# Joining the score matmuls of an attention pair: two of them wait for the exponentials that free both PSUM score tiles

## The chip, the cores and the metric

The kernel runs on one NeuronCore of a Trainium2 chip. The metric is the device time of one execution in microseconds (us). Three runs of the kernel before took 1133.21, 1135.22 and 1140.99 us; the median is 1135.22 us.

## What is computed

Causal attention in blocks of 64 positions, followed by a bilinear feed-forward layer (FFN). There are 8 batches of 8 heads with 576 positions of 64 dimensions. All arrays are float32.

```python
scores = scale * np.matmul(q, k.transpose(0, 1, 3, 2))
mask = block_i >= block_j                       # blocks of 64 positions
scores = np.where(mask, scores, -1000000000.0)
attn = np.exp(scores - np.max(scores, axis=-1, keepdims=True))
attn = attn / (np.sum(attn, axis=-1, keepdims=True) + 1e-09)
x = (attn @ v).transpose(0, 2, 1, 3).reshape(B * S, H * D)   # 4608 x 512
out = (x @ w_a) * (x @ w_b) @ w_out             # 512 -> 1536 -> 512
```

## The kernel before, in words

**Pairs.** Attention works on pairs of heads: 32 pairs, four to a batch. The two heads of a pair lie on partitions 0 to 63 and 64 to 127, so each score matmul has 64 rows (line 542). From pair 10 on (`NATIVE`), each float32 product is made of three matmuls of split operands; before, it is one float32 product.

**Score tiles.** The queries of a pair fall into four tiles of 128, numbered 0 to 3 (`LAST` is 3), and one block that is called the side tile (`NT`). Their scores live in two PSUM tiles, `x` and `y`, of two banks each, and there is one buffer of each (`ps_sc`, line 304):

- C3 writes score tile 3 to `x`, and C1 writes score tile 1 and the side tile to `y`;
- C2 writes score tile 2 to `x` once it is free again, and C0 writes score tile 0 to `y`.

**Exponentials.** VectorE takes the row maxima (t3, t4, t1, t2, t0; line 568), ScalarE the exponentials (line 595). There are two instructions for each tile, one per head: e3, e4 (the side tile), e1, then e2 and e0. C2 may overwrite `x` when e3 is done; C0 may overwrite `y` when e1 and e4 are done. C3 of the next pair needs `x` back from e2, and its C1 needs `y` back from e0.

**After the exponentials.** VectorE sums and inverts (rc, line 658 and below), GpSimd normalises (line 683), VectorE transposes in blocks (lines 688 and 693), DMAs rearrange (`at`, line 739), and TensorE multiplies by the values (V, line 748, 60 matmuls of 64 output columns). V of pair p waits for C0 of pair p+2, so it is placed right behind it. ScalarE copies the result out and splits it (X, H), GpSimd makes the low part (S).

**The FFN's first pass** on a batch needs S of the batch's four pairs. It runs in two halves of a batch. A half has 96 matmuls for the products with `w_a` and `w_b`, and 48 for the output products of the half before it (line 261, 128 x 128 by 128 x 288). They are issued in groups of four (`mm4`) and fill TensorE wherever attention leaves it free. When the attention's 32 pairs and 14 of these halves are through, `rest()` issues the last batch's halves and the output products that are left. The second pass (line 1160) takes the rest of the time, from about 583 us on.

**The order** of the instructions on every engine is written out by `plan()` ahead of time, from estimated durations (`TOOK`, `LAGS`). It takes the engine and operation that can start first; among the operations that are ready within `look` it takes the smallest key. Attention's keys lie near the slot of the pair (`SLOTS`: 12.0 us for each of the first 12 pairs, 15.2 us after), and an FFN group's key is 1e6, so that groups of the FFN only fill. C3 of a pair can't be planned ahead of the start of its slot (`at=B0`). Every operation on TensorE has a `mode`: 0 for the FFN, transposes and warm-up matmuls, 1 for scores, 2 for V; a change of mode costs `SWITCH` in the plan. The order is fixed once it is planned; on the chip the engines follow it, and semaphores hold the real dependencies.

These lines carry the waits that matter here:

```python
add("C3", PE_, ..., [("ql", p), ("kl", p), ("e3" if single_next else "e2", p - 1)], 0, at=B0, mode=1, ...)
add("C1", PE_, c1, [("C3", p, -LAGS[PE_]), ("ql2", p), *([...] if single_next else [("e0", p - 1)])], 0.1, mode=1, ...)
add("C2", PE_, ..., [("e3", p), ("C1", p, -LAGS[PE_])], 7.0, mode=1, ...)
add("C0", PE_, ..., [("C2", p, -LAGS[PE_]), ("e1", p), ("e4", p)], 7.1, mode=1, ...)
```

Of the kernel before, what the change touches and what calls it, by code (L numbers as in the profile page):

```python
# [35 lines left out]
K2 = 2  # L36
FIRST = 8
WARM_P = 2
PET = 6
A_KEY = 12  # L40
SLOTS = [12.0] * 12 + [15.2] * 20
CONV_AT = [0, 6.8, 13.6, 20.4, 28.2, 36, 43.8, 51.6, 59.4, 67.2, 75, 82.8]
CONV_KEY = 12.0
CONV_LO = True
KEEP_UNTIL, KEEP_EVERY = 66.0, 2.5
SWITCH = 0.1
LAGS = {"PE": 0.24, "DVE": 0.14, "Activation": 0.17, "Pool": 0.1, "SP": 2.0}
TOOK = {
# [41 lines left out]
def attention_then_bilinear_ffn(  # L90
# [222 lines left out]
    nk = [min(P * t + 3 * BLK, S - BLK) for t in range(NT)]  # L313
    ew = [min(P * (t + 2), S - BLK) for t in range(NT)]
    LAST = NT - 1
# [47 lines left out]
    PE_, DVE_, ACT_, POOL_, SP_ = LAGS  # L363
# [12 lines left out]
    def plan(look=0.0):  # L376
        free = dict.fromkeys(LAGS, 0.0)
        ready = {e: [] for e in LAGS}
        users = [[] for _ in ops]
        left = [len(o.deps) for o in ops]  # L380
        for o in ops:
            for d, plus in o.deps:
                users[d.n].append((o, plus))
            if not o.deps:
                ready[o.eng].append(o)
        out = []
        mode = 0
        bus = 0.0
        held = []

        def since(o):
            if not o.frees:
                return o.at
            if len(held) < MM:
                return o.at
            r = held[-MM]
            return o.at if r is o else 1e9 if r.end is None else max(o.at, r.end)

        while any(ready.values()):
            t, e = min((max(free[e], min(map(since, q))), e) for e, q in ready.items() if q)  # L400
            o = min((o for o in ready[e] if since(o) <= t + look), key=lambda o: (o.key, o.n))
            t = max(t, since(o))
            if o.frees:
                held.append(o.frees)
            ready[e].remove(o)
            free[e] = t + o.took + (SWITCH if e == PE_ and o.mode != mode else 0)
            if e == PE_:
                mode = o.mode
            if o.also:
                free[ACT_] = max(free[ACT_], t) + o.also  # L410
            o.start, o.end = t, free[e] + o.lag
            if o.kind in KB:
                bus = max(bus, t + LATENCY - 0.3) + KB[o.kind] / RATE
                o.end = bus + 0.3
            out.append(o)
            for u, plus in users[o.n]:
                u.at = max(u.at, o.end + plus + (SLACK if u.eng == PE_ and e != PE_ else 0))
                left[u.n] -= 1
                if not left[u.n]:
                    ready[u.eng].append(u)  # L420
        assert len(out) == len(ops)
        return out
# [23 lines left out]
    def ends(x):  # L446

        return x.rearrange("p (c k) -> p c k", k=BLK)[:, ::S // BLK - 1]

    def products(p, x, y):  # L450

        if p < NATIVE:
            return [(x[:, 0], y[:, 0])]
        x, y = x.bitcast(F32R), y.bitcast(F32R)
        return [(x[:, 1], y[:, 1]), (x[:, 1], y[:, 0]), (x[:, 0], y[:, 1])]

    base = [sum(SLOTS[:p]) for p in range(len(SLOTS))]
    done = {}

    def got(what, p):  # L460
        return done.get((what, p))

    def attention(p):
# [5 lines left out]
        B0 = base[p]  # L469
# [5 lines left out]
        def add(what, eng, fn, deps=(), off=0.0, kind=None, **kw):  # L475
            deps = [(got(*d[:2]), *d[2:]) if isinstance(d, tuple) else (d,) for d in deps]
            done[what, p] = o = Op(kind or what, eng, fn, [(*d, 0.0)[:2] for d in deps if d[0]], key=B0 + off, **kw)
            return o
# [44 lines left out]
        def bank(x):  # L523
            st[x] = ps_sc.tile([P, 2, 512], F32, tag=x, name=f"{x}{n}_{len(st)}")
            return st[x]
# [11 lines left out]
        def scores(t, out):  # L537
            qk = products(p, heads[p]["q"], heads[p]["k"])
            for j, (qq, kk) in enumerate(qk):
                for h, r in enumerate(rows):  # L540
                    keys = ends(kk[r]) if t == NT else kk[r, :nk[t]]
                    nc.tensor.matmul(  # L542
                        out[h] if isinstance(out, list) else out[:, h], qq[r, q0[t]:q0[t] + P], keys, start=j == 0,
                        stop=j == len(qk) - 1 and not (masked and t != LAST), skip_group_check=masked)
            if masked and t != LAST:
                for h, r in enumerate(rows):
                    to = out[h] if isinstance(out, list) else out[:, h]
                    to, val = (to, neg[r]) if t == NT else (to[:, nk[t] - BLK:nk[t]], neg[r, BLK:])
                    nc.tensor.matmul(to, who[r], val, start=False, stop=True, skip_group_check=True)

        single_next = p and p - 1 < SINGLE
        nat = "m" if masked else "n" if native else ""
        side = slice(nk[1], nk[1] + P)

        def c1():
            y = bank("y")
            scores(NT, y[:, :, side])
            scores(1, y[:, :, :nk[1]])

        add("C3", PE_, lambda: scores(LAST, bank("x")), [("ql", p), ("kl", p), ("e3" if single_next else "e2", p - 1)], 0, at=B0, mode=1, kind=nat + "C3")  # L560
        add("C1", PE_, c1, [("C3", p, -LAGS[PE_]), ("ql2", p), *([("e4", p - 1), ("e1", p - 1)] if single_next else [("e0", p - 1)])], 0.1, mode=1, kind=nat + "C1")

        def tile_small():
# [56 lines left out]
        if single:  # L620
            c1_ = ("C1", p, -LAGS[PE_])
            r2 = Op("none", PE_, lambda: ring(2, 0), [(got("C1", p), -LAGS[PE_])], key=B0 + K2)

            def c2():
                ring(2, 1)
                scores(2, [view(2, h) for h in range(2)])

            o2 = add("C2", PE_, c2, [(r2, 0.0), c1_], K2 + .01, mode=1, kind=nat + "C2")
            def c0():
                ring(0, 1)  # L630
                st[0, 0] = ps_sc.tile([P, 512], F32, tag="av", name=f"s{n}_0_0")
                scores(0, [view(0, h) for h in range(2)])

            o0 = add("C0", PE_, c0, [("C2", p, -LAGS[PE_]), ("X", p - 1)], K2 + .1, mode=1, kind=nat + "C0")
            add("t2", DVE_, lambda: [nc.vector.tensor_reduce(st["nm"][:, h, 2:3], view(2, h), axis=AX.X, op=ALU.max, negate=True) for h in range(2)], [("C2", p), ("t3", p)], K2 + 1, kind="u2")
            add("t0", DVE_, lambda: [nc.vector.tensor_reduce(st["nm"][:, h, :1], view(0, h), axis=AX.X, op=ALU.max, negate=True) for h in range(2)], [("C0", p), ("t3", p)], K2 + 1.2, kind="u0")
        else:
            add("C2", PE_, lambda: scores(2, bank("x")[:, :, :nk[2]]), [("e3", p), ("C1", p, -LAGS[PE_])], 7.0, mode=1, kind=nat + "C2")
            add("C0", PE_, lambda: scores(0, bank("y")[:, :, :nk[0]]),
                [("C2", p, -LAGS[PE_]), ("e1", p), ("e4", p)], 7.1, mode=1, kind=nat + "C0")  # L640
            if masked:
                done["m2", p] = got("C2", p)
            else:
                add("m2", DVE_, lambda: mask(2, "x"), [("C2", p)], 8.0)
            add("t2", DVE_, lambda: top(2, st["x"][:, :, :nk[2]]), [("m2", p)], 8.1)
            if masked:
                done["m0", p] = got("C0", p)
            else:
                add("m0", DVE_, lambda: mask(0, "y"), [("C0", p)], 8.2)
            add("t0", DVE_, lambda: top(0, st["y"][:, :, :nk[0]]), [("m0", p)], 8.3)  # L650
# [72 lines left out]
        for i, t in enumerate((LAST, 2, 1, 0, NT)):  # L723
            for h in range(2):
                prev = add("N", POOL_, lambda t=t, h=h: norm(t, h), [prev, got("rc", p)], 13 + i, kind=f"N{t}")
                if by_pe:
                    o = add("T", PE_, lambda t=t, h=h: pe_turn(t, h), [prev, ("V0", p - 1, -LAGS[PE_])], 14 + i, kind=f"P{t}")
                    o.frees = add("A", ACT_, lambda t=t, h=h: place(t, h), [o, *at_free], A_KEY + i, kind=f"A{t}")
                    ts.append(o.frees)
# [7 lines left out]
        def move(i, g):  # L737
# [4 lines left out]
                 key=B0 + 23) for i in range(NQ) for g in range(NQ)]  # L742
# [27 lines left out]
        for c in range(NCH):  # L770
            o = add("V", PE_, lambda c=c: values(c), vs, 18 if by_pe else 27, mode=2, kind=f"V{c}")
# [241 lines left out]
    while k * KEEP_EVERY < KEEP_UNTIL:  # L1013
        o = Op("keep", PE_, keep_on, at=4 + k * KEEP_EVERY, key=1e5)
# [14 lines left out]
    o = Op("st", SP_, start_conv2, [done["C0", NP - 1], done["V", NP - 1]], key=base[-1] + 10)  # L1029
    for k in range(EARLY):  # L1030
        o = Op("cv1", DVE_, lambda: next(box["g"]), [o, done["rc", NP - 1]], key=base[-1] + 20 + k)
# [526 lines left out]
```

## Time and profile before

| | before |
|---|---|
| median of three runs | 1135.22 us (1133.21 to 1140.99) |
| span of the profiled execution, first to last instruction | 1131.4 us |
| mean granted TensorE clock | 0.997 of full speed |
| TensorE matmul, busy | 1106.5 us, 98% of the span |
| VectorE, busy | 867.4 us, 77% |
| ScalarE, busy | 634.7 us, 56% |
| GpSimd, busy | 407.0 us, 36% |
| last V of the attention ends | 522.6 us |

How to read the profile. PE is TensorE's matmul, PEld its loading of weights, DVE is VectorE, ACT ScalarE, POOL GpSimd, SP the queue that issues most DMAs. A row of the timeline gives the start in us, the time that the row covers, the engine, the line, the operation, output and inputs, and the shape; neighbours of one kind are merged (`x6`). Matmuls are pipelined and their ends are modelled, so two neighbours overlap in the rows: what a piece of work costs TensorE is read from the start of its first matmul to the start of the next piece. For the profiled execution the page gives the span and no other time, so the sum of the prediction is made against the span, and the median lies 3.8 us above it.

### The profile page before, as it was taken

Reading aid. Unit: us, or ns where it says so; the run is one execution under the profiler, and the core shown is the slowest. Engines: PE = TensorE matmul, PEld = TensorE weight load, DVE = VectorE, ACT = ScalarE, POOL = GpSimd, SP = SyncE. Lnnn points to the kernel's source line nnn. Section 1 sums busy time; section 2 is a strip of 40 time slices with the busy share of each in tenths; the row PEclk is TensorE's granted clock in tenths of the full one; section 3 lists DMA queues with packets and bytes.
Section 4 is the critical chain, followed back from the end, with each engine's and each line's share of the span. In section 5 each row is a group of like instructions: output and inputs, shape, how many; then the busy total and the mean of one; then the engine's idle time right before and its main releaser. Section 6 shows DMA issues by size and latency. Waiting matters only on the chain.

```text
span 1131.4 us, 23204 instructions
## 1 busy us (share of the span) xinstructions
PE 1106.5 (98%) x8441; PEld 1040.2 (92%) x8441; DVE 867.4 (77%) x1797; ACT 634.7 (56%) x1632; POOL 407.0 (36%) x602
## 2 busy tenths in 40 slices
PE   8899999999999999999999999999999999999998
PEld 5567888899989998999999999999999999999998
DVE  6877878687678777753999997787874867867857
ACT  6877576566666556643465554545543545545532
POOL 4876667566656667551100120211202112022020
PEclk9999999999999999999999999999999999999999
DMA  5542688888777877857242663845669135055151
GB/s 171 156 145 87 168 242 217 226 227 213 205 222 210 223 210 201 240 159 209 90 146 73 181 179 86 215 121 144 181 217 333 37 76 112 17 96 102 26 98 56
DMA packets 78257, 178.74 MB, mean 158 GB/s; under 512 B 13120, under 2 KB 34624, under 8 KB 78144
## 3 DMA queue, kind: packets, MB, share of 16 engines
q1 hardware_dynamic: 65472, 159.95, 47.2%
q0 software_dynamic: 12672, 17.31, 10.2%
q8 instruction: 67, 1.10, 0.4%
q14 instruction: 46, 0.38, 0.1%
HBM read 80.74 MB, written 48.76 MB: 114 GB/s over the span
## 4 chain that ended last, share of the span: by engine, by line
PE 78%; DVE 6%; DMA 5%; ACT 4%; POOL 3%; SPq 3%; issue 2%; DVEq 0%; ACTq 0%; POOLq 0%
PE bank L1160 47%; PE ps L261 13%; PE pso L261 6%; PE av L748 5%; PE x L542 3%; PE y L542 2%; SPq L739 2%; ACT e L595 2%; POOL e L683 1%; DMA at<-bl 1%; DVE bl L688 1%; DMA qr<-qT 1%; DVE nm L568 1%; PE tp L709 1%; DMA kr<-kT 1%
## 5 line engine op out<-in xcount | busy, mean ns | idle before, releaser
L1160 PE MATMUL bank<-xh,wab 128*128 128x384 f32 x1344 | 350.0, 338 | 0.7 <-DVE t L1077 0.7
L1266 POOL DMA_DIRECT2D outT<-pt x88 | 78.0, 1129 | 468.6 <-ACT pt L1413 277.6
L1160 PEld LDWEIGHTS bank<-xh,wab 128*128 128x128 f32 x1344 | 244.7, 187 | 1.4 <-DVE t L1077 1.0
L1160 PE MATMUL bank<-xl,wab 128*128 128x384 f32 x672 | 227.0, 338 | 0.0
L261 PE MATMUL ps<-xh,wab 128*128 128x288 f32 x1024 | 213.9, 298 | 0.4 <-ACT ob L873 0.3
L261 PEld LDWEIGHTS ps<-xh,wab 128*128 128x128 f32 x1024 | 165.8, 188 | 6.4 <-issue 4.3
L683 POOL TENSOR_SCALAR e<-e,rc 128x512 f32<-128x512 f32 (+3 forms) x256 | 152.7, 616 | 45.3 <-DVE rc L663 45.3
L261 PE MATMUL ps<-xl,wab 128*128 128x288 f32 x512 | 153.3, 299 | 0.0
L1160 PEld LDWEIGHTS bank<-xl,wab 128*128 128x128 f32 x672 | 125.9, 187 | 0.0
L1077 DVE TENSOR_TENSOR u<-bank,u 128x384 f32<-128x384 f32 x156 | 86.7, 556 | 48.4 <-PE bank L1160 45.2
L688 DVE STREAM_TRANSPOSE bl<-e 128x512 f32<-128x512 f32 (+1 forms) x208 | 110.2, 582 | 10.4 <-POOL e L683 8.7
L1160 PE MATMUL bank<-hz,wo 128*128 128x384 f32 x612 | 110.0, 334 | 0.0
L1160 PEld LDWEIGHTS bank<-hz,wo 128*128 128x128 f32 x612 | 106.5, 188 | 0.0
L748 PEld LDWEIGHTS av<-at,v 128*64 128x64 f32 x1920 | 92.2, 137 | 10.3 <-issue 5.0
L748 PE MATMUL av<-at,v 128*64 128x128 f32 (+1 forms) x1920 | 97.2, 258 | 3.9 <-DMA at<-bl 2.7
L261 PE MATMUL pso<-hh,wo 128*128 128x288 f32 x480 | 100.9, 298 | 0.0
L261 PEld LDWEIGHTS ps<-xl,wab 128*128 128x128 f32 x512 | 96.1, 188 | 3.8 <-issue 3.2
L1077 DVE TENSOR_TENSOR t<-bank,t 128x384 f32<-128x384 f32 x96 | 53.3, 556 | 40.5 <-ACT t L1203 20.3
L261 PEld LDWEIGHTS pso<-hh,wo 128*128 128x128 f32 x480 | 77.6, 188 | 4.4 <-issue 4.1
L595 ACT ACTIVATE e<-y,nm 128x320 f32<-128x320 f32 (+1 forms) x126 | 60.9, 487 | 28.3 <-DVE nm L568 22.4
L568 DVE TENSOR_REDUCE nm<-x 128x2 f32<-128x1024 f32 (+1 forms) x63 | 72.1, 1145 | 5.7 <-PE x L542 4.5
L849 POOL TENSOR_TENSOR hl<-hf,hh 128x288 fp32r<-128x288 f32 x56 | 46.2, 825 | 84.0 <-ACT hh L845 81.6
(156 smaller groups left out, 2006.6 us busy)
## 6 DMA issues: line engine op xcount, KB each, us to landing
at<-bl SPq DMA_DIRECT2D x416, 112.0 KB, 2.5
xr<-xd SPq DMA_DIRECT2D x48, 384.0 KB, 4.6
outT<-pt POOLq DMA_DIRECT2D x88, 192.0 KB, 6.4
cv<-wab SPq DMA_DIRECT2D x24, 512.0 KB, 5.5
v<-vm SPq DMA_DIRECT2D x32, 320.0 KB, 3.5
xd<-xf SPq DMA_DIRECT2D x32, 288.0 KB, 2.6
outT<-ob SPq DMA_DIRECT2D x64, 144.0 KB, 2.3
wabd<-st SPq DMA_DIRECT2D x8, 896.0 KB, 5.3
```

The source lines that it names most:

```text
L261: nc.tensor.matmul(ps, w_, d_, start=(i == 0), stop=(i == n - 1))
L542: nc.tensor.matmul(out[h] if isinstance(out, list) else out[:, h], qq[r, q0[t]:q0[t] + P], keys, start=j == 0, stop=j == len(qk) - 1 and n ...
L568: nc.vector.tensor_reduce(st["nm"][:, :, t], view, axis=AX.X, op=ALU.max, negate=True)
L595: nc.scalar.activation(out, src, AF.Exp, bias=bias, accum_out=sm[:, h, t, :1])
L683: nc.gpsimd.tensor_scalar(ev, ev, st["rc"][:, h, t:t + 1], 1.0, op0=ALU.mult, op1=ALU.mult)
L688: nc.vector.transpose(dst, es[h][t].rearrange("p (c g q) -> p c g q", g=NQ, q=QB))
L739: nc.sync.dma_start(st["at"][QB * g:QB * (g + 1), i], bl[QB * i:QB * (i + 1), g])
L748: nc.tensor.matmul(out[d], v[:, h, c], a[:, qs, h, e_], start=start, stop=stop, skip_group_check=True)
L849: nc.gpsimd.tensor_tensor(lo, box2["hf"], f32(hi), op=ALU.subtract)
L1077: return lambda: v.tensor_tensor(o, a, b, op=op)
L1160: nc.tensor.matmul(banks[bk], a, b, start=start and not i, stop=i == 3 * n - 1, skip_group_check=not start)
L1266: do("acc", POOL_, lambda: nc.gpsimd.dma_start(part[o * P:(o + 1) * P, ts], t, accum_op=ALU.add), [name], [("part", o, 2 * tt_ + j)], key= ...
```

## The change

- From pair 8 on (`JOIN`), C2 waits for e1 and e4 as well as for e3, and C3 waits for e0 of the pair before as well as for e2. C2 and C0 then become ready together, and so do C3 and C1.
- In `plan()`, when TensorE is in mode 1 or 2, an operation with a mode that can start within 0.3 us (`STAY`) is taken ahead of anything else, for all pairs.
- The planned cost of a change of mode goes from 0.1 to 0.2 us (`SWITCH`).
- Within C1, score tile 1 comes ahead of the side tile; it was the other way round.
- For pair 0, a dependency is written without its plus of 0.0; that is the same dependency.

```diff
+JOIN = 8
+STAY = 0.3
...
-SWITCH = 0.1
+SWITCH = 0.2
...
             t, e = min((max(free[e], min(map(since, q))), e) for e, q in ready.items() if q)
-            o = min((o for o in ready[e] if since(o) <= t + look), key=lambda o: (o.key, o.n))
+            stay = [o for o in ready[e] if o.mode and since(o) <= t + STAY] if e == PE_ and mode else []
+            o = min(stay or (o for o in ready[e] if since(o) <= t + look), key=lambda o: (o.key, o.n))
...
         def c1():
             y = bank("y")
+            scores(1, y[:, :, :nk[1]])
             scores(NT, y[:, :, side])
-            scores(1, y[:, :, :nk[1]])
...
-        add("C3", PE_, lambda: scores(LAST, bank("x")), [("ql", p), ("kl", p), ("e3" if single_next else "e2", p - 1)], 0, at=B0, mode=1, kind=nat + "C3")
+        add("C3", PE_, lambda: scores(LAST, bank("x")), [("ql", p), ("kl", p), ("e3" if single_next else "e2", p - 1), *([("e0", p - 1)] if p >= JOIN else [])], 0, at=B0, mode=1, kind=nat + "C3")
...
-            o2 = add("C2", PE_, c2, [(r2, 0.0), c1_], K2 + .01, mode=1, kind=nat + "C2")
+            o2 = add("C2", PE_, c2, [r2, c1_], K2 + .01, mode=1, kind=nat + "C2")
...
-            add("C2", PE_, lambda: scores(2, bank("x")[:, :, :nk[2]]), [("e3", p), ("C1", p, -LAGS[PE_])], 7.0, mode=1, kind=nat + "C2")
+            add("C2", PE_, lambda: scores(2, bank("x")[:, :, :nk[2]]), [("e3", p), *([("e1", p), ("e4", p)] if p >= JOIN else []), ("C1", p, -LAGS[PE_])], 7.0, mode=1, kind=nat + "C2")
```

## The prediction, made before the changed kernel ran

> **What bounds the kernel now.** I read the page first: TensorE's matmuls cover 98% of the span, the other engines far less.
>
> ```profile
> span 1131.4 us, 23204 instructions
> PE 1106.5 (98%) x8441; PEld 1040.2 (92%) x8441; DVE 867.4 (77%) x1797; ACT 634.7 (56%) x1632; POOL 407.0 (36%) x602
> ```
>
> So time is won where TensorE needs less for the same work, or idles less. The modelled ends hide what a matmul costs, so the second view is TensorE's timeline, read from start to start. These rows are pair 20's C2 (`x`), one FFN group, and C0 (`y`).
>
> ```profile
> 313.59 0.43 PE L261 MATMUL ps<-xh,wab 128*128 128x288 f32 x2
> ...
> 313.99 0.43 PE L261 MATMUL ps<-xh,wab 128*128 128x288 f32 x2
> 314.35 0.87 PE L542 MATMUL x<-k,q 64*128 64x448 f32 x6
> 315.15 0.40 PE L261 MATMUL ps<-xl,wab 128*128 128x288 f32 x1
> ...
> 315.87 0.58 PE L542 MATMUL y<-k,q 64*128 64x192 f32 x6
> 316.38 0.78 PE L748 MATMUL av<-at,v 128*64 128x64 f32 x12
> ```
>
> In a stream, three FFN matmuls take 0.40 us (313.59 to 313.99), 0.133 each, so a group of four is worth 0.53. Alone between C2 and C0 it takes 0.72: 0.19 more. C2 takes 0.80 and C0 0.51. Pair 11 is one of three where C0 follows C2 directly:
>
> ```profile
> 173.47 0.87 PE L542 MATMUL x<-k,q 64*128 64x448 f32 x6
> 174.18 0.48 PE L542 MATMUL y<-k,q 64*128 64x192 f32 x6
> 174.58 0.53 PE L261 MATMUL ps<-xh,wab 128*128 128x288 f32 x2
> ```
>
> There C2 takes 0.71 and C0 0.40. Split, the three pieces take 0.80 + 0.72 + 0.51 = 2.03; joined they are worth 0.71 + 0.40 + 0.53 = 1.64. **A split between C2 and C0 costs TensorE 0.39 us**: 0.20 in the scores, 0.19 in the FFN piece.
>
> The Trainium skill has a rule against this: by "TensorE: Matmul & The Clock Gate", section "Step-by-step: what each phase is for", the drain of one matmul overlaps the fill of the next, so neighbours are N cycles apart. By that rule alone the order of the pieces costs nothing and the sum below is 0. The trace disagrees, with 0.72 against 0.53 us for the same four matmuls. It sides with the skill's "TensorEngine Tiling (Array Packing)", section "Key Properties": a change of tiling mode drains TensorE.
>
> **The change part by part.** *C2 joined to C0.* Of pairs 8 to 31, an FFN piece stands between C2 and C0 in 21 (all but 11, 30 and 31). The pieces of the first and the last of them, pairs 8 and 29, begin so:
>
> ```profile
> 130.12 0.40 PE L261 MATMUL pso<-hl,wo 128*128 128x288 f32 x1
> ...
> 456.49 0.40 PE L261 MATMUL ps<-xl,wab 128*128 128x288 f32 x1
> ```
>
> No FFN matmul goes; it only moves into a longer stream. The gain is 21 x 0.39 = 8.2 us; I use pair 20's price for pieces of any length, since it belongs to the seams.
>
> *C3 joined to C1.* They are adjacent in most pairs already. FFN stands between them in pairs 11 and 22 only (V in pair 9). Pair 20, then pair 22:
>
> ```profile
> 303.03 3.13 PE L748 MATMUL av<-at,v 128*64 128x64 f32 x60
> 306.09 0.96 PE L542 MATMUL x<-k,q 64*128 64x512 f32 x6
> 306.89 0.93 PE L542 MATMUL y<-k,q 64*128 64x128 f32 x12
> 307.75 0.40 PE L261 MATMUL ps<-xl,wab 128*128 128x288 f32 x1
> ```
>
> ```profile
> 337.05 0.96 PE L542 MATMUL x<-k,q 64*128 64x512 f32 x6
> 337.94 0.53 PE L261 MATMUL pso<-hh,wo 128*128 128x288 f32 x2
> ...
> 338.66 1.04 PE L542 MATMUL y<-k,q 64*128 64x128 f32 x12
> 339.63 0.40 PE L261 MATMUL pso<-hh,wo 128*128 128x288 f32 x1
> ```
>
> Split: 0.89 + 0.72 + 0.97 = 2.58. Joined: 0.80 + 0.86, and 0.53 for the group, 2.19. Again 0.39; two pairs give 0.8 us.
>
> *What the later C3 loses.* In seven pairs, such as 20 above, C3 follows V directly. If C3 waits for e0 too, V will be done first and a piece of FFN will come between, at the 0.19 of a lone piece. V and scores have different shapes (128\*64 and 64\*128), so the seam behind V is paid either way. 7 x 0.19 = 1.3 us lost; the bounds are 0 and, if all 24 pairs that have none today got one, 4.6.
>
> *The new waits.* TensorE takes its instructions in order, so behind a C2 that waits stand C0, V and the FFN; the plan is to fill the time before it with FFN groups instead. What is left of such waits now:
>
> ```profile
> PEld x L542 <- ACT e L595: 5.9, 14, 1.6
> ```
>
> That is 0.42 us each time. The 24 C2 and 24 C3 of the change could each wait so (20 us, 14 more than now), or none (5.9 less). I take no difference: the plan leaves the same spare time ahead of a C2 that waits for e1 as ahead of one that waits for e3.
>
> *The other edits.* `STAY` and `SWITCH` act on pairs 0 to 7 too. There I take nothing, because TensorE waits for work rather than work for TensorE (the FFN row below, first window); what that cover may be worth if it is gone is the 8 matmuls of that row, 1 us either way. The order within C1 changes which shape meets the FFN: at most the 0.10 that an exit to FFN showed in either score tile (C2 0.80 against 0.71), 32 times, 3 us either way; nothing taken, since the number of matmuls and of seams is the same. No DMA, and nothing on SP's or POOL's queue, is added; they shift with the pair.
>
> *How much later the pair gets.* This is the cost side, and the third view: pair 21 on ScalarE and VectorE.
>
> ```profile
> 328.93 0.20 ACT L595 ACTIVATION_READ_ACCUMULATOR e<-x,nb 128x1 f32 x1
> 330.91 0.23 ACT L595 ACTIVATION_READ_ACCUMULATOR e<-y,nm 128x1 f32 x1
> 331.10 0.60 DVE L693 STREAM_TRANSPOSE bl<-e_s 64x128 f32<-64x128 f32 x2
> 331.73 0.17 DVE L580 MEMSET x<- 64x128 f32 x1
> 331.93 1.09 DVE L568 TENSOR_REDUCE nm<-x 128x2 f32<-128x896 f32 x1
> ...
> 337.46 0.24 ACT L595 ACTIVATION_READ_ACCUMULATOR e<-y,nm 128x1 f32 x1
> ```
>
> e3 ends at 329.13, e1 at 331.14: C2 becomes ready 2.0 us later. It started at 329.78 and will start near 331.3, so its scores are there near 332.1 and t2 starts near 332.4. VectorE was at transposes until 331.70 and started t2 only at 331.93; so of the 1.5 us, 0.5 reach t2, e2 and e0. Then the second wait: e0 ended at 337.70, 0.65 after C3 of pair 22 had started. With the 0.5, and some 0.3 for the group in progress, C3 starts near 338.5, **1.4 us later**. With VectorE free it would be 1.5 + 0.65 + 0.3 = 2.4; where C3 comes long after e0 it is 0, as from pair 12 (e0 ended at 191.71) to pair 13:
>
> ```profile
> 191.49 0.22 ACT L595 ACTIVATION_READ_ACCUMULATOR e<-y,nm 128x1 f32 x1
> ...
> 195.72 0.96 PE L542 MATMUL x<-k,q 64*128 64x512 f32 x6
> ```
>
> Does lateness add up? C3 of pairs 12, 14, 15 and 31:
>
> ```profile
> 179.00 0.96 PE L542 MATMUL x<-k,q 64*128 64x512 f32 x6
> ...
> 213.28 0.96 PE L542 MATMUL x<-k,q 64*128 64x512 f32 x6
> ...
> 227.33 0.96 PE L542 MATMUL x<-k,q 64*128 64x512 f32 x6
> ...
> 477.83 0.96 PE L542 MATMUL x<-k,q 64*128 64x512 f32 x6
> ```
>
> From 12 to 31 a pair takes 298.83 / 19 = 15.73 us, but from 14 to 15, behind a late C3, 14.05. 14.05 + 1.4 = 15.45 is still under 15.73. So between 0 and 2.4 us a pair I take 0: most pairs can make the delay good within their time.
>
> *What lateness would cost.* Nothing while there is FFN to fill with. These windows count its matmuls up to the end of pair 7's V, to that of pair 31's, and after:
>
> ```profile
> 0.00:150.34 150.34, 35.30 (x232) 31.45 (x232) 0.98 0.50 152
> 150.34:522.58 372.24, 232.18 (x1620) 216.59 (x1620) 1.00 0.77 211
> 522.58:1131.40 608.82, 54.23 (x404) 53.53 (x404) 1.00 0.48 127
> ```
>
> The plan holds 14 halves of 144 less the last 48, 1968. Before pair 7's values only 96 + 144 = 240 of them can run, and 232 have: 8 left. When pair 31's V ends, 232 + 1620 = 1852 have run and 116 are left (of the 404 after it, 288 are the last batch's), 15.4 us, or 0.64 us for each of 24 pairs. The joined scores use up 0.39 of this, since TensorE gets through the FFN faster. **The pair may get 0.25 us slower on average at no cost**; each further 0.1 us costs 2.4 us.
>
> **Sum**: 8.2 + 0.8 - 1.3 = 7.7 us less. Against the span that is 1131.4 - 7.7 = 1123.7; the median of the runs lies 3.8 above the span, so **1127.5 us**. "Within 1%" means 1123.9 to 1146.6, about what a measurement of this kernel can tell from no change.
>
> **The rivals.**
> - *Starved TensorE, slower.* The two waits lengthen the chain of a pair, and TensorE runs out of FFN ahead of pair 11's, 15's, ... 31's V. It costs nothing up to 0.25 us a pair, eats the gain at 0.25 + 7.7 / 24 = 0.57, and is over 1% slower from about 1.05. At pair 21's 1.4 for all: (1.4 - 0.25) x 24 = 27.6 lost, 1155. For it: C3 did start before e0's end there, and pairs with less to make good have no slack. Against it: 14.05, and the 4.0 us from pair 12 to 13. Chance 0.14, mostly 1143 to 1155.
> - *The gain is given back.* The lag lies between 0.25 and 0.57, or new waits of 0.42 at a third of the 48 joins (7 us) take the seams' place: 1131 to 1139. For it: 14 such waits exist already. Against it: they are 5.9 us in 400. Chance 0.22.
> - *Seams cost nothing.* What I read as 0.39 is weight loading and waiting that turns up wherever the piece goes. Then 1135. The skill's overlap rule above is this case. Against it: 2.03 against 1.64 for the same work. Also here: C2 and C0 don't come together at all. Chance 0.04.
> - *More than the sum.* FFN pieces between V and C3 (eleven pairs) go as well, 2.1 us, the 1.3 isn't lost, and waits for exponentials shrink by half, 3 us: 1121. Chance 0.10.
> - *The forecast*, 1124 to 1131: chance 0.50, of which 0.05 touches the faster side.
>
> **Chances and range.** Faster by over 1%: 0.10 + 0.05 = 0.15. Slower by over 1%: most of the first rival, 0.13. Within: 0.72. The range from 1121 to 1143 leaves out the first rival and a little below.
>
> **What the changed profile would show.** C0's rows right behind C2's, with C2 at 0.70 and C0 at 0.40 to 0.51, in all of pairs 8 to 31; C2 starting after e1, C3 after e0; about 7 more FFN pieces between V and C3; waits of the scores for ACT near 6 us; pairs at 15.4 to 15.9 us; at pair 31's V some 1850 FFN matmuls done, and that V ending near 515. From there on nothing should change. I am wrong if idle time of TensorE ahead of scores, or of an FFN group that waits for a low part, grows by several us, or if a pair takes over 16 us.

## The result, and the profile after

The changed kernel is slower: median 1151.13 us of four runs (1148.0 to 1154.93) against 1134.48 (1133.21 to 1140.99) before; the ratio is 1.0127, with a 95% interval from 1.0088 to 1.0166. The forecast was 1127.5, with a range to 1143.

The page of the changed kernel, its first lines and the group of the matmuls that write `x` (behind the bar: busy time, mean ns, idle time ahead of them and what ended it):

```profile
span 1148.6 us, 23202 instructions
PE 1106.3 (96%) x8441; PEld 1050.6 (91%) x8441; DVE 858.2 (75%) x1797; ACT 630.0 (55%) x1632; POOL 405.6 (35%) x602
L545 PE MATMUL x<-k,q 64*128 64x512 f32 (+1 forms) x340 | 62.1, 463 | 15.7 <-ACT e L598 12.4
```

TensorE is busy for as long as before (1106.5), but the span is 17.2 us longer. Outside its matmuls it spends 42.3 us (1148.6 - 1106.3) instead of 24.9; the largest part stands in the last line. **The seams went as forecast.** The timeline of pair 20's C2 and C0:

```profile
337.06 0.88 PE L545 MATMUL x<-k,q 64*128 64x448 f32 x6
337.77 0.48 PE L545 MATMUL y<-k,q 64*128 64x192 f32 x6
338.19 0.67 PE L751 MATMUL av<-at,v 128*64 128x64 f32 x10
```

C2 takes 0.71 and C0 0.42 from start to start, and no FFN stands between them in any of pairs 8 to 31 (the median from C2's start to C0's is 0.72 us). From C3 of pair 8 on, TensorE's FFN comes in 48 pieces instead of 73.

**What came in their place** are waits. The waits of TensorE (total us, times, longest), after and then before:

```profile
PE x L545 <- ACT e L598: 12.4, 8, 3.4
PE y L545 <- ACT e L598: 4.3, 5, 1.4
...
PEld x L545 <- ACT e L598: 14.9, 12, 3.6
```

```profile
PE x L542 <- ACT e L595: 2.6, 5, 1.4
```

On the matmuls they go from 2.6 to 16.7 us. In the row that the prediction showed, that of the weight loads for `x`, 5.9 us in 14 waits became 14.9 in 12: not more waits, but longer ones. In the timeline of the changed kernel the two longest look so; the bracket gives the idle time and what ended it:

```profile
152.01 2.99 PE L751 MATMUL av<-at,v 128*64 128x64 f32 x60
158.45 0.96 PE L545 MATMUL x<-k,q 64*128 64x512 f32 x6 [3.44 <-ACT e L598]
```

```profile
325.79 0.98 PE L545 MATMUL x<-k,q 64*128 64x512 f32 x6 [2.32 <-ACT e L598]
```

At 158.45 there is nothing to fill with. The FFN's matmuls in windows that end with pair 7's V, with pair 31's V, and with the span:

```profile
0.00:154.90 154.90, 35.97 (x240) 33.07 (x240) 0.97 0.48 148
154.90:550.90 396.00, 244.49 (x1728) 233.99 (x1728) 0.99 0.73 200
550.90:1148.60 597.70, 38.99 (x288) 38.30 (x288) 1.00 0.49 128
```

All 240 that can run have run at the end of pair 7's V, and all 1968 at the end of pair 31's: no FFN is in reserve, where before there were 8 and 116. Between them, at the V of pairs 11, 15, 19, 23 and 27, the reserve is 16, 0, 16, 16 and 16, where before it was 56, 92, 100, 100 and 132 (counted in the timelines, as in the windows). The FFN also stands elsewhere: ahead of C2, which now comes later, there are 59.6 matmuls a pair instead of 42.3, and between C2 and the next C3 only 12.0 instead of 25.3 (means of pairs 12 to 30). Of the 13.5 us that scores wait in these pairs, 8.5 are C3's. This is the picture of the rival "starved TensorE". The experiments show that it is not the main cause: in e8 below the reserve is used up in the same way, and the loss is 0.5% instead of 1.3%.

**Where the 17.2 us are.** The second pass (`bank`) starts at 597.07 instead of 583.31: 13.8 us. Of these, 4.8 are lost before any wait is joined: C3 of pair 8 starts at 126.68 instead of 121.89 (two profiles of one kernel, e4 and e17 below, differ by 3.2 at that place). The other 3.4 are lost at the start of the second pass:

```profile
PE bank L1163 <- DVE xl L1115: 2.0, 2, 1.2
PEld bank L1163 <- DVE xl L1115: 2.6, 2, 1.6
```

Before, no matmul of the second pass waits for `xl`. VectorE prepares the second pass while TensorE works off the last FFN matmuls; with 288 left after pair 31's V instead of 404 it has 15 us less for this.

### The profile page after: what moved, and what is told of

The parts are those of the page before. It is cut to its first block, busy times and chain, and to the rows that moved or that the text cites. A ratio compares the mean times of both kernels' runs of the same rounds, so it can differ in the third digit from the quotient of the medians.

```text
span 1148.6 us, 23202 instructions
## 1 busy us (share of the span) xinstructions
PE 1106.3 (96%) x8441; PEld 1050.6 (91%) x8441; DVE 858.2 (75%) x1797; ACT 630.0 (55%) x1632; POOL 405.6 (35%) x602
## 4 chain that ended last, share of the span: by engine, by line
PE 67%; DVE 12%; ACT 6%; DMA 6%; SPq 3%; POOL 3%; issue 3%; ACTq 0%; DVEq 0%; POOLq 0%
PE bank L1163 46%; PE ps L263 8%; PE pso L263 5%; PE av L751 3%; ACT e L598 3%; DVE bl L691 3%; SPq L742 2%; DMA at<-bl 2%; PE x L545 2%; DVE nm L571 2%; PE y L545 2%; DMA qr<-qT 1%; POOL e L686 1%; ACT at L718 1%; DMA xr<-xd 1%
## 5 line engine op out<-in xcount | busy, mean ns | idle before, releaser
L263 PE MATMUL ps<-xh,wab 128*128 128x288 f32 x1024 | 216.9, 302 | 0.2 <-DVE hf L844 0.2
L263 PEld LDWEIGHTS ps<-xh,wab 128*128 128x128 f32 x1024 | 169.0, 192 | 3.4 <-PE y L545 0.8
L691 DVE STREAM_TRANSPOSE bl<-e 128x512 f32<-128x512 f32 (+1 forms) x208 | 112.0, 583 | 21.1 <-POOL e L686 13.8
L263 PE MATMUL pso<-hh,wo 128*128 128x288 f32 x480 | 98.4, 295 | 0.0
L545 PE MATMUL x<-k,q 64*128 64x512 f32 (+1 forms) x340 | 62.1, 463 | 15.7 <-ACT e L598 12.4
```

The costliest lines, as they stand in the source:

```text
L263: nc.tensor.matmul(ps, w_, d_, start=(i == 0), stop=(i == n - 1))
L545: nc.tensor.matmul(out[h] if isinstance(out, list) else out[:, h], qq[r, q0[t]:q0[t] + P], keys, start=j == 0, stop=j == len(qk) - 1 and n ...
L691: nc.vector.transpose(dst, es[h][t].rearrange("p (c g q) -> p c g q", g=NQ, q=QB))
```

## The experiments

**First: the joins or the planning?** The edits, each against the kernel that the expectation names (e1 to e4 with an underscore are runs; without one, exponentials):

```diff
# e1_no_join, in the changed kernel
-JOIN = 8
+JOIN = 99
# e2_join_only, in the kernel before: both of these; e3_c2_only: the second; e4_c3_only: the first
-[..., ("e3" if single_next else "e2", p - 1)]                                                   # C3
+[..., ("e3" if single_next else "e2", p - 1), *([("e0", p - 1)] if p >= JOIN else [])]
-[("e3", p), ("C1", p, -LAGS[PE_])]                                                              # C2
+[("e3", p), *([("e1", p), ("e4", p)] if p >= JOIN else []), ("C1", p, -LAGS[PE_])]
```

> The changed kernel with JOIN at 99: no pair's waits are joined, STAY, SWITCH and the order within C1 stay as changed. Theory A (the joined waits lengthen the chain of a pair by 0.9 us and starve TensorE): the loss of 17 us goes for the most part, 1133 to 1139, a pair from 12 to 31 takes 15.6 to 15.9 us, and the FFN count at pair 31's V is again 100 or more below 1968. Theory B (the planning edits STAY and SWITCH make the order worse): it stays slow, 1146 to 1152, with a pair near 16.6.

> The kernel before with JOIN = 8 alone (C2 waits for e1 and e4, C3 for e0), without STAY, SWITCH at 0.1 and the old order within C1. Theory A: 1143 to 1152, a pair takes 16.3 to 16.8 us, FFN used up at each batch's last V. Theory B: 1127 to 1136, a pair stays near 15.7.

> The kernel before with the wait of C2 for e1 and e4 alone, from pair 8 on. Theory A, by the sums of the two traces (from e3 to e2 2.0 us more, from e2 to e0's end 0.9 less): this wait is the one that lengthens the chain; 1141 to 1152, a pair at 16.3 to 16.7. A rival, that C3's wait for e0 is what lengthens it: near before, 1128 to 1137.

> The kernel before with the wait of C3 for e0 alone, from pair 8 on. Theory A (C3 has slack, since e3 waits for VectorE's transposes of the pair before and not for C3): 1132 to 1138, a pair near 15.7. The rival (C3's wait lengthens the chain): 1143 or more, a pair over 16.2.

| kernel | median us | ratio to before, 95% interval | us a pair, 12 to 31 |
|---|---|---|---|
| e1_no_join | 1162.91 | 1.0218 (1.0174 to 1.0262) | 16.86 |
| e2_join_only | 1141.18 | 1.0031 (1.0003 to 1.0058) | 16.55 |
| e3_c2_only | 1141.04 | 1.0020 (0.9993 to 1.0047) | 16.50 |
| e4_c3_only | 1134.82 | 0.9973 (0.9951 to 0.9994) | 15.86 |

Each ratio is against the kernel before in the same round of runs; its median lay between 1134.5 and 1138.5 us in the rounds of this document.

My theory (A) fell on the first row: without any joined wait the kernel is slower still, and beyond what theory B expected, too. The joins alone cost 0.3%, less than A expected and more than B, though the time of a pair and the used-up reserve are as A had them. It is C2's wait that does it, by the time of a pair (16.50; the interval of the ratio reaches below 1); C3's alone gains a little. The planning edits do the greater harm, and they did it without starving TensorE: e1_no_join has 116 FFN matmuls left at pair 31's V, as before.

**Second: which planning edit?**

```diff
# e5_switch_only, in the kernel before
-SWITCH = 0.1
+SWITCH = 0.2
# e6_stay_only, in the kernel before
-            o = min((o for o in ready[e] if since(o) <= t + look), key=lambda o: (o.key, o.n))
+            stay = [o for o in ready[e] if o.mode and since(o) <= t + STAY] if e == PE_ and mode else []
+            o = min(stay or (o for o in ready[e] if since(o) <= t + look), key=lambda o: (o.key, o.n))
# e7_no_stay, in the changed kernel: the reverse of that
# e8_switch_back, in the changed kernel
-SWITCH = 0.2
+SWITCH = 0.1
```

> The kernel before with SWITCH at 0.2 alone. Theory C (a dearer switch stretches TensorE's planned time, so the plan puts fewer FFN groups ahead of a score tile than the chip needs to cover the exponentials, and TensorE stalls there): 1142 to 1160, waits of the scores for ACT of 20 us or more against 10.7 before, and fewer than 42 FFN matmuls between C1 and C2 of a pair. Theory D (STAY alone does the harm): 1130 to 1139, waits near 10.

> The kernel before with STAY at 0.3 alone (with the order of pair 0's first ring tile made explicit, as in the changed kernel). Theory D (the plan holds TensorE for a score tile or V that should come within 0.3 us, and on the chip it comes later): 1142 to 1160, waits of scores and V for ACT and DMA well over those before. Theory C: 1130 to 1139.

> The changed kernel with STAY taken out: joined waits, SWITCH at 0.2, new order within C1. Theory D: 1137 to 1143, as with the joined waits alone (1141). Theory C: it keeps most of the loss, 1146 to 1156.

> The changed kernel with SWITCH back at 0.1: joined waits, STAY at 0.3, new order within C1. Theory C: 1137 to 1143, as with the joined waits alone. Theory D: it keeps most of the loss, 1146 to 1156.

| kernel | median us | ratio to before, 95% interval | us a pair, 12 to 31 |
|---|---|---|---|
| e5_switch_only | 1157.17 | 1.0198 (1.0164 to 1.0231) | 16.30 |
| e6_stay_only | 1136.06 | 0.9998 (0.9978 to 1.0018) | 15.87 |
| e7_no_stay | 1156.05 | 1.0183 (1.0158 to 1.0208) | 16.84 |
| e8_switch_back | 1140.97 | 1.0049 (1.0029 to 1.0069) | 16.52 |

It is `SWITCH`, a number that changes no work and no wait, only the order. `STAY` does nothing alone. With `SWITCH` back, what remains of the loss is that of the joins.

The effects don't add up. `SWITCH` costs 2.0% alone, but 0.8% in the changed kernel (1.0127 against 1.0049). The joins cost 0.3% to 0.5% with `SWITCH` at 0.1, but with `SWITCH` at 0.2 and `STAY` they gain 0.9% (1.0218 without them, 1.0127 with them). Of the joins, `STAY` and `SWITCH`, `SWITCH` is the only one that makes the changed kernel faster when it alone is taken back.

**Third: why?** `SWITCH` adds to TensorE's time in the plan. Either that price is at fault, or any longer planned time.

```diff
# e9_group_long, in the kernel before
-"mm4": (0.528, 0.24, 0)
+"mm4": (0.564, 0.24, 0)
# e10_switch_slack, in the kernel before
-SWITCH = 0.1
+SWITCH = 0.2
-SLACK = 0.3
+SLACK = 0.7
# e11_switch_zero, in the kernel before
-SWITCH = 0.1
+SWITCH = 0.0
# e12_c1_order, in the kernel before
-            scores(NT, y[:, :, side])
             scores(1, y[:, :, :nk[1]])
+            scores(NT, y[:, :, side])
# e13_switch_comp, in the kernel before
-SWITCH = 0.1
+SWITCH = 0.2
-"mm4": (0.528, 0.24, 0)
+"mm4": (0.480, 0.24, 0)
```

> The kernel before with the planned time of an FFN group of four at 0.564 us in place of 0.528 (18 groups a pair, 0.65 us more of planned TensorE time a pair, about what SWITCH at 0.2 adds), SWITCH at 0.1. The chip's work is unchanged but for its order. Theory C (any longer planned TensorE time makes the plan bring scores too early against the exponentials, and TensorE stalls): 1145 to 1162, waits of the scores for e over 20 us. Rival E (it is the price of a switch that makes the plan choose a bad sequence): 1131 to 1140.

> The kernel before with SWITCH at 0.2 and SLACK at 0.7 in place of 0.3 (0.4 us more of planned spare time ahead of every TensorE operation that waits for another engine). Theory C in its narrow form (the stalls come from too little spare time): back to 1134 to 1146, waits of scores for e below 15 us. Rival F (the order on ScalarE and VectorE gets worse, spare time on TensorE doesn't mend it): 1148 to 1162.

> The kernel before with SWITCH at 0. Theory C: as fast as before or faster, 1126 to 1137, waits of scores for e below 10 us. Rival (the order needs a true price of the seams; 0.1 was the better of two errors): 1140 to 1155, with more pieces of FFN between scores.

> The kernel before with score tile 1 ahead of the side tile in C1 and nothing else. The order of the plan is the same. All theories: no change that can be measured, 1131 to 1139; the prediction bounded it at 3 us either way.

> The kernel before with SWITCH at 0.2 and the planned time of an FFN group at 0.480 in place of 0.528, so that TensorE's planned time for a pair is about what it was (18 groups x 0.048 = 0.86 us less against some seven switches x 0.1 more). Theory C2 (what hurts is a longer planned TensorE time, from whichever term, since the plan then puts less FFN between a pair's scores than the chip has time for): 1132 to 1143, with 67 or more FFN matmuls in a pair of pairs 12 to 31. Theory E (the price of a switch hurts by itself): 1148 to 1162.

| kernel | median us | ratio to before, 95% interval | us a pair, 12 to 31 |
|---|---|---|---|
| e9_group_long | 1157.02 | 1.0180 (1.0148 to 1.0212) | 16.22 |
| e10_switch_slack | 1163.01 | 1.0228 (1.0186 to 1.0270) | 16.79 |
| e11_switch_zero | 1141.58 | 1.0044 (1.0026 to 1.0062) | 16.14 |
| e12_c1_order | 1135.47 | 0.9988 (0.9966 to 1.0010) | 15.89 |
| e13_switch_comp | 1136.26 | 0.9995 (0.9966 to 1.0023) | 15.80 |

e9 loses as much as e5 with the old `SWITCH`; e13, with the dearer switch and a cheaper FFN group, loses nothing. So it is the planned time of TensorE as a whole and not the price of a switch by itself; a shorter planned time for the FFN group alone was not run. The profile says in part how. Waits of the scores in the whole run for ScalarE, and the FFN matmuls between C3 of pair 12 and C3 of pair 31, for e5, e9 and e13, and these matmuls before:

```profile
PE x L542 <- ACT e L595: 16.7, 14, 3.2
...
PE y L542 <- ACT e L595: 1.0, 2, 0.6
```

```profile
189.40:499.00 309.60, 182.86 (x1257) 169.50 (x1256) 0.99 0.76 208
```

```profile
PE x L542 <- ACT e L595: 9.1, 12, 2.0
PE y L542 <- ACT e L595: 4.3, 3, 2.4
```

```profile
184.20:492.40 308.20, 180.39 (x1241) 166.06 (x1240) 1.00 0.77 211
```

```profile
PE x L542 <- ACT e L595: 5.7, 7, 3.3
...
PE y L542 <- ACT e L595: 1.6, 2, 1.4
```

```profile
183.60:483.90 300.30, 188.46 (x1308) 176.19 (x1308) 0.99 0.79 216
```

```profile
178.90:477.80 298.90, 184.92 (x1286) 171.82 (x1284) 1.00 0.79 218
```

In e5 and e9, with a longer planned time, 29 and 45 fewer FFN matmuls stand in these 19 pairs, and of the waits above 9.5 and 9.1 us fall into them; in e13 no fewer matmuls, and 1.6 us, against 2.0 before. The loss of e5 is in waits and the clock: outside its matmuls TensorE spends 45.1 us instead of 24.9, and the mean granted clock falls from 0.997 to 0.991, an estimated 7 us of the span; that is 27 of the 28.1 us that the span is longer. Some 7 of them are lost before pair 8 (its C3 starts at 129.08 instead of 121.89). And FFN lies ready meanwhile. In e5, up to pair 23's V:

```profile
0.00:407.30 407.30, 178.50 (x1220) 164.30 (x1220) 0.98 0.66 188
```

240 + 4 x 288 = 1392 could have run, 1220 had: 172 in reserve, more than before, while TensorE stood in front of a score tile that the order puts first. The kernel before plans a group at what it takes in a stream (0.528 us) and a switch at about half of what it costs, so its order holds more FFN for the planned time than TensorE gets through in it; that this surplus covers the time in which ScalarE is late is argued from these counts and not shown. It fits e9, where 36.2 FFN matmuls a pair stand ahead of C2 in place of 42.3 (means of pairs 12 to 30). In e5 there are 41.7, nearly as many as before, so there later exponentials probably weigh more.

The narrow form of this failed: e10 adds planned spare time ahead of TensorE's waits and loses no less (1.0228; the interval overlaps with e5's), 13 us of it already by pair 8 (C3 of pair 8 starts at 134.9 instead of 121.9). e11 shows that no price at all is worse too, which theory C did not expect; there TensorE's matmuls are busy for 8.7 us longer (1115.2) and its time outside them grows by 2.7 only. So 0.1 is the best of the three prices tried. Which of ScalarE's and VectorE's instructions move in the plan to make their part later (in e5, from the end of e0 to the next pair's e3 takes 7.55 us on average, 6.65 before) is left open.

**Fourth: do joins pay while FFN is in reserve?**

```diff
# e14_join20: as e2_join_only; e15_c2_from20: as e3_c2_only; both with
-JOIN = 8
+JOIN = 20
# e16_after_mended, in the changed kernel
-JOIN = 8
+JOIN = 20
-SWITCH = 0.2
+SWITCH = 0.1
# e17_c3_again: e4_c3_only, in more rounds
```

> The kernel before with JOIN = 20: both joined waits, but only from pair 20 on, where 100 FFN matmuls are in reserve. Theory A2 (a join saves TensorE 0.39 us as long as FFN is in reserve, and the longer pair is harmless until it is used up): splits go in 11 pairs, C3 loses its place behind V in five; 3 us less in TensorE's work, given back in part at the end, where the reserve is used up: 1130 to 1136 where before is 1135.5, and no FFN matmul missing before pair 31's V. Rival (the join costs whatever the reserve, by waits): 1138 to 1144.

> The kernel before with C2's wait for e1 and e4 alone, from pair 20 on. Theory A2: ten splits of 0.39 us go, some seams come back, and a little of the reserve stays at the end: 1129 to 1135 where before is 1135.5. Rival (the join costs by waits): 1138 to 1144.

> The changed kernel with two numbers altered: SWITCH back at 0.1, and JOIN = 20, so that pairs are joined only where FFN is in reserve. STAY and the order within C1 stay as changed. If the loss has the two causes found (a longer planned TensorE time; the reserve of FFN used up), neither is left, and the joins may show: 1129 to 1136, 0.994 to 1.000 of before. If STAY or the joins cost by themselves: 1138 to 1144.

> Once more the kernel before with C3's wait for e0 alone, from pair 8 on, in more rounds: it was the only kernel whose interval lay below 1 (0.9973, 0.9951 to 0.9994). If that gain is real: 0.995 to 0.999 again. If it was chance: an interval that reaches over 1.

| kernel | median us | ratio to before, 95% interval | FFN left at pair 31's V |
|---|---|---|---|
| e2_join_only, for comparison | 1141.18 | 1.0031 (1.0003 to 1.0058) | 0 |
| e14_join20 | 1135.99 | 0.9980 (0.9955 to 1.0005) | 0 |
| e15_c2_from20 | 1135.19 | 0.9984 (0.9956 to 1.0012) | 16 |
| e16_after_mended | 1134.31 | 0.9991 (0.9975 to 1.0007) | 0 |
| e17_c3_again | 1134.23 | 0.9974 (0.9953 to 0.9995) | 84 |

Joined from pair 20 on, nothing is lost, and the gain of some 2 us is within the interval of no change. e14 and e16 use up the whole reserve and pay at the start of the second pass (from its start to the end 551.9 and 551.6 us, against 548.1 before); their second pass starts at 583.0 and 580.5, against 583.3 before, which is no proof of a gain, as e4 and e17, one kernel, differ by 2.9 us there. With its two numbers mended, the changed kernel is as fast as before, so `SWITCH` and the reserve that the joins of pairs 8 to 19 use up early account for the loss. If it were the joins by themselves, 12 joined pairs should cost half of what 24 cost in e8, a ratio of 1.0025; that lies outside e16's interval. C3's later wait alone came out below before twice: 0.9973 and 0.9974, both intervals below 1. That is about 3 us; the intervals of e14 to e16 overlap with it, so it is not shown to be the best version. Its windows, as above:

```profile
0.00:526.00 526.00, 272.60 (x1884) 253.31 (x1884) 0.99 0.69 194
526.00:1130.70 604.70, 49.85 (x372) 49.33 (x372) 1.00 0.48 127
```

## Why the prediction was wrong, by its steps

**The step that failed most: "The other edits. `STAY` and `SWITCH` act on pairs 0 to 7 too. There I take nothing".** `STAY` and C1's order were indeed nothing (0.9998, 0.9988). `SWITCH` was priced at 1 us either way, for the early pairs alone; it costs 2.0% alone, and 0.8% in the changed kernel (11.2 us between the two profiled spans, 1148.6 and 1137.4 in e8). In the early pairs alone it was about 5 us in these profiles: with `SWITCH` back, C3 of pair 8 starts at 121.68 instead of 126.68. I had weighed the seams against the chip, where 0.2 a switch is near the truth (0.39 for two), and not what a truer price does to the order.

**"The new waits: I take no difference."** They went from 2.6 to 16.7 us, at the upper bound that I gave (14 more), which was also one of my signs of being wrong. The reason given, equal spare time in the plan, was no reason: the joined waits are not even waits on the chip. C3 of pair 20 starts at 325.79 and e0 ends at 326.14. The semaphores hold C3 for e2 only (it ends at 325.74); e0 was a date for the plan. Of pairs 8 to 31, C3 starts before that e0 ends in 17, and C2 before e1 ends in 10.

**"How much later the pair gets: between 0 and 2.4 us a pair I take 0."** It was 0.94 (0.82 with the joins alone). C3 of pairs 12 and 31 in the changed kernel:

```profile
192.41 0.96 PE L545 MATMUL x<-k,q 64*128 64x512 f32 x6
...
509.04 0.96 PE L545 MATMUL x<-k,q 64*128 64x512 f32 x6
```

316.63 / 19 = 16.66 us against 15.73. Means over pairs 12 to 30, from the starts and ends of the instructions in the two traces:

| us | before | after |
|---|---|---|
| C3 to the start of e3 | 5.66 | 6.82 |
| start of e3 to start of e2 | 5.52 | 7.49 |
| start of e2 to end of e0 | 3.64 | 2.74 |
| end of e0 to the next C3 | 0.91 | -0.39 |
| sum | 15.73 | 16.66 |

The term that was too small is C2's delay. In pair 21 I had read that C2 becomes ready 2.0 us later, and let 0.5 of it through to e2, because VectorE was at transposes until then. On average all of it arrives: from the start of e3 to that of e2 it takes 1.97 us more, with C2's joined wait alone (e3_c2_only) 1.86 more, and with C3's alone (e4_c3_only) nothing. Behind e2, 0.90 us is made good up to the end of e0, and hardly more after it. From the end of e0 to the next pair's e3 it takes 6.65 us before and 6.52 in the changed kernel (the rows of the table, 0.91 + 5.66 and -0.39 + 6.82, give 6.57 and 6.43, since they begin with another pair), though C3 starts 1.30 us earlier against e0. Between the two VectorE has rc and the transposes of the old pair, in the order of their keys, ahead of the new pair's t4 and nb, so an earlier C3 need not bring e3 forward. With `SWITCH` at 0.1 more is made good there: in e2_join_only and e3_c2_only, with C3 0.11 and 0.40 us before the end of e0, e3 follows e0 by 6.08 and 5.71. How far C3's place sets the time of a pair is left open. The 14.05 us from pair 14 to 15 was one pair whose C3 had been late; it was no proof that pairs can run so on average.

**Right**: the seam's price; the 21 and 2 splits that go; that lateness costs when the reserve is spent (e2_join_only, e8); the supply of 240 and 288. The price can be checked where the joins stand with `SWITCH` at 0.1: TensorE's busy time falls by 4.4 us in e2_join_only and 5.4 in e8, at a mean clock of 0.994 and 0.995 instead of 0.997. With an estimated 3.4 and 2.3 us for the clock, that is near the 7.7 of the sum. The pieces of FFN fell by 25 and not by the 16 of 21 + 2 - 7. The bound of 4.6 us counted 24 pairs without a piece ahead of C3, but only the seven named had none. **Not priced**: the 3.4 us at the start of the second pass when the reserve is 0. By the first rival's own sum, 0.94 a pair would have cost (0.94 - 0.25) x 24 - 7.7 = 8.9 us; its mechanism was in the traces, but it had 0.14 of the chance and there was a larger one beside it.

One sentence of the description was also wrong: the dependency of pair 0 that loses its 0.0 is not the same one. With the 0.0 it stood in a pair of brackets that was looked up as a name and dropped; the change makes it hold. It orders two operations of pair 0. e6 holds this edit too, and is as fast as before.

## What to carry to other kernels

Where an order is written from estimated durations, an estimate that is too cheap on the busiest engine can be what keeps that engine supplied: a truer value can cost time, so time it alone, as an edit of its own. Before work is delayed to save seams, find the chain that really sets the period, by the averages of each step over many iterations, and count what is in reserve to fill with; the saving lasts only while that reserve does. A gap before one instruction is no slack for the whole until a run shows that filling it leaves the period as it was.

## What the runs showed of the hardware that was not expected

A wait of TensorE can cost more than itself. The granted clock (the third number from the right) around the two waits shown above, and behind a third, in the changed kernel:

```profile
161.00:164.00 3.00, 3.00 (x16) 3.00 (x17) 2.71 (x9) 0.22 (x1) 3.00 (x6) 0.64 0.53 127
...
326.00:329.00 3.00, 3.00 (x23) 2.76 (x22) 1.93 (x5) 1.69 (x7) 2.11 (x3) 0.67 0.28 102
...
460.00:464.00 4.00, 4.00 (x20) 4.00 (x20) 3.66 (x9) 0.57 (x2) 4.00 (x7) 0.57 0.81 217
```

Before, the whole stretch of pairs 8 to 31 ran at full clock:

```profile
121.90:522.60 400.70, 393.98 (x3994) 358.45 (x3993) 293.35 (x684) 242.49 (x772) 241.51 (x371) 1.00 0.77 211
```

The FFN's 60 matmuls behind the wait at 325.79 took 9.33 us, where 60 behind pair 21's C1, in the same kernel, took 8.19. The third dip comes behind a wait of 1.70 us that ends at 458.30. Not every wait has one: behind waits of 1.82 and 1.64 us, from 290.8 and 390.1 on, the clock stayed full, and so it did behind one of 2.54 us in e2_join_only.

Three such dips in this stretch and one more among the early pairs than before help to close the account. TensorE spends 17.4 us more outside its matmuls (42.3 against 24.9). The dips add 4 x 1.1 = 4.4 us by the piece measured, or an estimated 6.9 by the mean clock of the span (0.991 against 0.997). The seams take 7.7 off. That makes 14.1 to 16.6 of the 17.2 us. The Trainium skill, "TensorE: Matmul & The Clock Gate", section "What's actually happening", gives the cold clock after at least one idle window of some 3.4 us. Here waits of 2.32 and 1.70 us among work were followed by a dip, so a shorter gap can be enough; the measurement decides.
